# A retention, mixture-of-experts and gated-linear kernel: the first expert's last 64 tokens as stationary operand, and another order of the tile's products

## The chip, the cores and the metric

The kernel runs on one core of a Trainium2 chip. Its time is the device time of one launch in microseconds (us). Before the change three runs gave 780.53, 781.26 and 782.92 us; the median, 781.26 us, is the time to be predicted against. One further execution was profiled, and all rows below are from it.

The engines are named as in the profile: PE is TensorE (matmuls), PEld its loads of the stationary operand, DVE is VectorE, ACT ScalarE, POOL GpSimd, and SP issues most of the DMAs.

## The reference

Three stages follow each other on 2304 tokens (4 sequences of 576) with 512 features.

```python
# 1. retention: 8 heads of 64
scores = (1 / sqrt(64)) * q @ k.T
ret = scores * Dmat            # Dmat[i, j] = gamma_h ** (i - j) for i >= j, else 0
x = (ret @ v) rearranged to (2304, 512)
# 2. mixture of 8 experts, one expert for each token
do_compute = x @ w_skip > 0
e_idx = argmax(x @ w_gate)     # of the tokens with do_compute
gate_w = softmax probability of the chosen expert
h = maximum(x[mask] @ w1[e], 0)            # 512 -> 1024
y[mask] = gate_w * (h @ w2[e])             # 1024 -> 512
x[do_compute] += y
# 3. gated linear unit
out = ((x @ w_a) * (x @ w_b)) @ w_out      # 512 -> 1536 -> 512
```

All is computed in fp32. A fp32 matmul of the program is two matmul instructions in the trace, so that a count of the trace is twice a count of the program.

## The kernel before

**Retention.** The 2304 tokens are 18 tiles of 128 (two sequences are nine tiles: four of the first, four of the second, and one that holds the last 64 tokens of both). For each tile the loop issues, in this order: `scale_k(i + 2)` (POOL multiplies k by a decay, giving `ks`), `scores(i)` (PE, tile `s`; DVE masks them into `At`, L628), transposes of q for a later pair of tiles (`pq`, copied by DVE or ACT), transposes of k for the next tile (`pk`), `emit_x(i - 1)` (PE products `px` of the last tile's result with an identity and the gate's weights, then ACT copies and the store to `x_dram`), `state(i)` (PE product `psm` of k and v, eight 64 x 64 blocks; ACT adds it to the running state `mbd`), and `values(i)`. This last one has a carry part (`po<-qT,mbd`, L663, not in the first tile of a sequence, and L659 in the tile of two halves), an inner part (`po<-At,v`, L668), and a DVE multiplication into `xT`. The DMAs of tile i + 4 are issued behind it. In tiles 1, 6 and 15 a second q transpose stands between `state(i)` and `values(i)`.

`po` of the inner part and `psm` write 64 of the array's 128 columns with one instruction (128*64 in the trace) and `s` reads 64 of its rows (64*128); `pq`, `pk`, `px` and the carry part use the whole array (128*128).

**Routing and the first expert.** Behind some tiles DVE works out the route of the tokens (each expert takes up to `ROOM` = 192 of them). POOL gathers an expert's tokens as 128 and `REST` = 64 rows. The first 128 tokens of expert 0 are gathered from tiles 0 to 14 only, transposed in tile 17 ahead of `values(17)` by `turn_x(0, 0, ...)` (tile `xt`, copied by DVE to `xh`), and their eight first products (`steps`) are spread over the end of the retention, where the routing waits. `firsts` computes a block of 128 of the 1024 hidden features at a time: w1 is stationary (128 x 128), the tokens move. Behind tile 17 two steps run ahead of `emit_x(17)`. Two blocks of hidden features are copied out of PSUM with one ACT instruction (L487).

**Experts.** A branch that reads the number of extra rounds (L961, L962; none are taken with these inputs) follows. Then each expert's instructions are written out by a string of names: F0 to F7 are the first products, S0 to S7 the second ones of 128 tokens (`y`), Q0 to Q7 those of the 64 others (`yr`: tokens stationary, w2 moving in two halves, which go to the lower and the upper 64 columns of the array), X0 and X1 transposes of the next expert's tokens, E0 and E1 the stores, `N` a gather by POOL, `l` a load of expert weights, `tk` a scatter by POOL. `gs` starts and `gp` continues the conversion of a 512 KB piece of the gated unit's weights (ACT and DVE, `hb`, `mh`, `st`, `w`). For expert 0 only F (64 tokens) and Q are left there. All engines run their own instructions strictly in the order written.

**The gated unit** takes the last 400 us and is not touched.

Of the kernel before, what the change touches and what calls it, by code (L numbers as in the profile page):

```python
# [7 lines left out]
F32 = mybir.dt.float32  # L8
# [4 lines left out]
ACTF = mybir.ActivationFunctionType  # L13
# [5 lines left out]
P = 128  # L19
B, H, S, D = 4, 8, 576, 64  # L20
DM = H * D
NP = H // 2
NTOK = B * S
NT = NTOK // P
E = 8
KD = DM // P
F1 = 1024
F2 = 1536
CAP = 256
NBLK = E * CAP // P  # L30
ROOM = 192
# [33 lines left out]
def retention_moe_glu_kernel(  # L65
# [17 lines left out]
    nc = tc.nc  # L83
# [38 lines left out]
    ident = cst[:, C_ID:C_ID + P]  # L122
# [49 lines left out]
    def unit(u, k=3):  # L172
        assert ready.get(u, 0) > k, (u, ready.get(u))
        return units[u]
# [279 lines left out]
    REST = ROOM - P  # L454

    def turn_x(e, b, to, psum, engine):
        n = REST if b else P
        pt = psum([P, KD * n], "xt").rearrange("p (k n) -> p k n", k=KD)
        for kd in range(KD):
            nc.tensor.transpose(pt[:, kd], xg[e][:n, b, kd * P:(kd + 1) * P], ident[:n, :n])  # L460
        if engine is nc.scalar:
            nc.scalar.activation(out=to, in_=pt, func=ACTF.Copy)
        else:
            engine.tensor_copy(to, pt)

    def call(fn, *args):
        return lambda: fn(*args)
# [59 lines left out]
        return [call(second, f) for f in range(8)], finish  # L527


    experts = ExitStack()  # L530
    ps_k = experts.enter_context(tc.tile_pool(name="ps_k", bufs=1, space=PSUM))
    attn = ExitStack()
# [100 lines left out]
    def state(i):  # L633
        c = i % 9
        if c == 8:
            return
        if c % 4 == 0:
            mstate["ps"] = ps_o.tile([P, NP, P], F32, tag="m", name="psm")
        pm = mstate["ps"]
        for hp in range(NP):  # L640
            for r in range(2):
                part = slice(r * D, (r + 1) * D)
                nc.tensor.matmul(pm[part, hp, part], lhsT=ks_t[i][:, 2 * hp + r], rhs=qkv["v", i][:, 2 * hp + r],
                                 start=(c % 4 == 0 and hp == 0), stop=True, skip_group_check=True)
        m = mbd[2 + c // 4] if c % 4 == 3 else mbd[c % 2]
        for r in range(2):
            nc.scalar.activation(out=m[r * D:(r + 1) * D, :, r * D:(r + 1) * D],
                                 in_=pm[r * D:(r + 1) * D, :, r * D:(r + 1) * D], func=ACTF.Copy)
# [63 lines left out]
    for r in range(4):  # L712
# [5 lines left out]
                      in_=w_skip.rearrange("(a p o) -> p a o", p=P, o=1))  # L718
# [79 lines left out]
    for i in range(NT):  # L798
        scale_k(i + 2)
        scores(i)  # L800
        for job in q_jobs[i][:1]:
            q_transposes(*job)
        k_transposes(i + 1)
        emit_x(i - 1)
        state(i)
        route_at(i, "d")
        for job in q_jobs[i][1:]:
            q_transposes(*job)
        if i == NT - 1:
            tags = {"xt": (ps_o, "m"), "h0": (ps_s, "s0"), "h1": (ps_s, "s1"), "y": (ps_k, "o")}  # L810
            tiles = {"ht0": "v", "ht1": "k"}
            xh = at2.tile([P, KD, P], F32, tag="q", bufs=TBUFS["q"], name="xh")

            def early_psum(shape, n):
                return tags[n][0].tile(shape, F32, tag=tags[n][1], name=n)

            def early_sbuf(shape, dt, n):
                return xg[0][:, 0] if n == "yo" else at2.tile(shape, dt, tag=tiles[n], bufs=TBUFS[tiles[n]], name=n)

            ht_0 = {}  # L820
            fs = firsts(0, xh, P, 4, early_sbuf, early_psum, ht_0)
            ss, finish_0 = seconds(0, ht_0, early_sbuf, early_psum)
            steps = fs + ss
            turn_x(0, 0, xh, early_psum, nc.vector)
        values(i)
        load(i + 4)
        route_at(i, "e")
        if 7 <= i:
            for _ in range(1 if i < 14 else 2 if i < NT - 1 else 1):
                load_m()  # L830
        if i == 14:
            zeros = idle_bf.bitcast(F32)
            for j in range(0, ROOM, P):
                n = min(P, ROOM - j)
                for c in range(2):
                    nc.sync.dma_start(out=y_dram[YROWS - ROOM + j:YROWS - ROOM + j + n, c * 256:(c + 1) * 256],
                                      in_=zeros[:n])
    done = 2
    for go in steps[:done]:
        go()  # L840
    emit_x(NT - 1)
    for step, n in enumerate((5, 8, 11, 16)):
# [3 lines left out]
        done = n  # L846
# [115 lines left out]
    with tc.If(rounds > 0):  # L962
        with tc.tile_pool(name="o0", bufs=1) as o0:
            done = o0.tile([P, E], F32, name="done")
# [106 lines left out]
    def prepare_x(e, b):  # L1071
        if e == E:
            return
        if b == 0:
            xe[e] = m1.tile([P, KD, ROOM], F32, tag="xe", bufs=2, name="xe")
        turn_x(e, b, xe[e][:, :, P:] if b else xe[e][:, :, :P], m1_psum(e), nc.vector if b else nc.scalar)
# [6 lines left out]


    FIRST_PLAN = (
        "gs F0 gp F1 gp F2 gp F3 gs E0 F4 gp F5 gp X0 F6 gp F7 gs X1 N l l l l "
        "Q0 Q1 gp Q2 Q3 l l gp Q4 Q5 Q6 gp Q7 l l E1 "
    )
    PLAN = (
        "gs F0 gp F1 tk gp F2 gp F3 gs F4 tk gp F5 gp F6 gp F7 l l l l gs S0 S1 gp S2 "  # L1090
# [3 lines left out]
        "gs F0 f2 gp F1 f1 gp F2 f0 gp F3 gs F4 gp F5 gp F6 x1 gp F7 gs x2 S0 S1 gp t1 S2 "  # L1094
        "x0 S3 gp S4 t2 S5 gp s1 S6 t0 S7 E0 gs s2 Q0 Q1 s0 gp Q2 Q3 gp Q4 Q5 gp Q6 Q7 E1 gs "
    )
    xe = {}
    tokens_put = [0]

    def put_tokens():  # L1100
# [7 lines left out]
    def run_expert(e, plan):  # L1108
        sbuf, psum = m1_sbuf, m1_psum(e)
        acts, ht = {}, {}  # L1110
        if e:
            acts["F"] = firsts(e, xe[e], ROOM, 2, sbuf, psum, ht)
            acts["S"], end_0 = seconds(e, ht, sbuf, psum)
            at = P
        else:
            acts["F"] = firsts(0, xh, REST, 8, sbuf, psum, ht)
            end_0, at = finish_0, 0
        acts["Q"], end_1 = seconds_rest(e, ht, at, sbuf, psum)
        acts["E"] = [end_0, end_1]
        named = {  # L1120
            "N": lambda: gather_x(e + 2), "gp": piece_step,
            "gs": lambda: taken[0] < early and piece_start(),
            "L": piece_load, "l": load_m, "tk": put_tokens,
        }
        uses = {}
        by_tile = {"f": fetch_rows, "x": mix_rows, "t": turn_rows, "s": split_rows}
        for name in plan.split():
            if name in named:
                named[name]()
            elif name[0] == "X":  # L1130
                prepare_x(e + 1, int(name[1]))
            elif name[0] in by_tile:
                by_tile[name[0]](int(name[1]))
            else:
                n = int(name[1])
                acts[name[0]][n]()
                if name[0] in "FSQ":
                    us = [4 * e, 4 * e + 1] if name[0] == "F" else [4 * e + 2 + n // 4]
                    for u in us:
                        uses[u] = uses.get(u, 0) + 1  # L1140
                        if uses[u] == (4 if e == 0 and name[0] == "Q" else 8):
                            used.add(u)

    for e in range(E):
        run_expert(e, FIRST_PLAN if e == 0 else PLAN if e < E - 1 else LAST_PLAN)
    assert loaded["m"] == len(m_pieces)
    experts.close()

# [152 lines left out]
```

## Time and profile before

| what | value |
|---|---|
| median of three runs | 781.26 us |
| profiled execution, whole | 775.75 us |
| its span, first to last instruction | 774.0 us |
| mean granted TensorE clock | 0.986 |
| PE busy | 754.4 us (97%) |
| PEld busy | 662.5 us (86%) |
| DVE, ACT, POOL busy | 305.8, 230.5, 105.6 us |
| the chain that ended last | PE 77%, DVE 4% |

The span's times below count from its first instruction. A busy time of PE covers matmuls that wait in the pipeline, so it says little of how densely the array worked. The start of one group to the start of the next is the better measure of what a group costs. A granted clock of 1.00 in a stretch is 2.4 GHz and 0.50 is 1.2 GHz.

### The profile page before, as it was taken

Reading aid. Unit: us, or ns where it says so; the run is one execution under the profiler, and the core shown is the slowest. Engines: PE = TensorE matmul, PEld = TensorE weight load, DVE = VectorE, ACT = ScalarE, POOL = GpSimd, SP = SyncE. Lnnn points to the kernel's source line nnn. Section 1 sums busy time; section 2 is a strip of 40 time slices with the busy share of each in tenths; the row PEclk is TensorE's granted clock in tenths of the full one; section 3 lists DMA queues with packets and bytes.
Section 4 is the critical chain, followed back from the end, with each engine's and each line's share of the span. In section 5 each row is a group of like instructions: output and inputs, shape, how many; then the busy total and the mean of one; then the engine's idle time right before and its main releaser. Section 6 shows DMA issues by size and latency. Waiting matters only on the chain.

```text
span 774.0 us, 11861 instructions
## 1 busy us (share of the span) xinstructions
PE 754.4 (97%) x4797; PEld 662.5 (86%) x4797; DVE 305.8 (40%) x660; ACT 230.5 (30%) x485; POOL 105.6 (14%) x135
## 2 busy tenths in 40 slices
PE   7999989899999999999999999999999999999997
PEld 5888876877776667988999999999999999999996
DVE  4446664556655136894322221222123222322111
ACT  3444531345444134553221221121112121212111
POOL 1221111202222102140040004000400030001000
PEclk9999999599999999999999999999999999999999
DMA  9979993599898764451030003000301020001001
GB/s 223 228 181 264 254 299 117 180 351 322 304 316 308 260 191 157 130 185 33 1 96 26 1 1 111 13 1 0 123 1 28 14 81 1 1 1 42 1 0 42
DMA packets 89611, 94.61 MB, mean 122 GB/s; under 512 B 44881, under 2 KB 67025, under 8 KB 89554
## 3 DMA queue, kind: packets, MB, share of 16 engines
q1 hardware_dynamic: 84210, 78.06, 33.1%
q0 software_dynamic: 5344, 15.76, 6.4%
q8 instruction: 39, 0.64, 0.3%
q14 instruction: 18, 0.15, 0.1%
HBM read 80.80 MB, written 13.01 MB: 121 GB/s over the span
## 4 chain that ended last, share of the span: by engine, by line
PE 77%; DVE 4%; ACT 0%; issue 0%; POOL 0%; ACTq 0%; DVEq 0%
PE ab L1167 36%; PE o L1184 18%; PE h L484 11%; PE y L498 6%; PE yr L516 4%; PE pt L1050 1%; PE xt L460 1%; DVE w L233 1%; DVE mh L230 1%; DVE mh L225 1%; DVE w L237 0%; DVE hb L234 0%; DVE hb L223 0%; DVE a_sb L1172 0%; ACT gg L445 0%
## 5 line engine op out<-in xcount | busy, mean ns | idle before, releaser
L1167 PE MATMUL ab<-xt,w 128*128 128x384 f32 x1728 | 311.6, 336 | 0.0
L1167 PEld LDWEIGHTS ab<-xt,w 128*128 128x128 f32 x1728 | 301.8, 188 | 6.0 <-issue 0.4
L1184 PE MATMUL o<-w,gg 128*128 128x512 f32 x648 | 161.4, 393 | 1.8 <-ACT gg L445 0.9
L1172 DVE TENSOR_TENSOR a_sb<-ab,a_sb 128x384 f32<-128x384 f32 x72 | 40.1, 557 | 271.8 <-PE ab L1167 239.7
L1184 PEld LDWEIGHTS o<-w,gg 128*128 128x128 f32 x648 | 119.2, 188 | 24.1 <-ACT gg L445 1.8
L1171 ACT ACTIVATE a_sb<-ab 128x384 f32<-128x384 f32 x72 | 35.3, 490 | 174.3 <-PE ab L1167 170.4
L445 ACT ACTIVATE gg<-a_sb 128x384 fp32r<-128x384 f32 x72 | 37.8, 525 | 161.5 <-DVE a_sb L1172 161.5
L484 PEld LDWEIGHTS h<-xe,w 128*128 128x128 f32 x448 | 72.6, 190 | 2.7 <-issue 2.7
L484 PE MATMUL h<-xe,w 128*128 128x192 f32 x448 | 74.7, 328 | 0.0
L498 PE MATMUL y<-w,ht 128*128 128x512 f32 x128 | 59.5, 598 | 0.0
L426 POOL DMA_INDIRECT out_dram<-ob,turns x15 | 14.8, 989 | 310.3 <-ACT ob L1191 308.1
L446 DVE TENSOR_TENSOR gg<-a_sb,gg 128x384 fp32r<-128x384 f32 x68 | 38.0, 559 | 40.2 <-ACT gg L445 37.8
L498 PEld LDWEIGHTS y<-w,ht 128*128 128x128 f32 x128 | 22.8, 190 | 19.9 <-issue 19.2
L233 DVE TENSOR_TENSOR w<-hb,st 128x512 fp32r<-128x512 f32 x36 | 24.8, 690 | 30.5 <-ACT st L228 25.3
L227 ACT ACTIVATE hb<-hb,ebias 128x512 int32<-128x512 int32 x36 | 25.9, 718 | 35.1 <-DVE hb L223 34.8
L487 ACT ACTIVATE ht<-h 128x384 f32<-128x384 f32 (+2 forms) x36 | 16.3, 452 | 55.8 <-PE h L484 54.8
L420 POOL DMA_INDIRECT xg<-x_dram,list_i x15 | 14.7, 982 | 119.3 <-PE xt L460 99.7
L516 PE MATMUL yr<-w,ht 128*64 128x256 f32 x256 | 30.9, 396 | 0.0
L516 PEld LDWEIGHTS yr<-w,ht 128*64 128x64 f32 x256 | 18.3, 142 | 14.4 <-DVE mh L230 3.8
L581 POOL TENSOR_TENSOR ks<-k,cst_a 128x512 f32<-128x512 f32 x18 | 18.8, 1044 | 79.6 <-DMA k<-in_k_dram 64.3
L237 DVE TENSOR_TENSOR w<-mh,hb 128x512 fp32r<-128x512 f32 x36 | 24.4, 688 | 5.3 <-ACT mh L232 3.6
L628 DVE TENSOR_TENSOR At<-s,cst_a 128x512 f32<-128x512 f32 x36 | 23.1, 684 | 6.2 <-PE s L625 6.2
(146 smaller groups left out, 654.3 us busy)
## 6 DMA issues: line engine op xcount, KB each, us to landing
w<-in_moe_w_dram SPq DMA_DIRECT2D x64, 512.0 KB, 6.7
st<-in_moe_w_a_dram SPq DMA_DIRECT2D x12, 512.0 KB
st<-in_moe_w_b_dram SPq DMA_DIRECT2D x12, 512.0 KB, 8.4
st<-in_moe_w_out_dram SPq DMA_DIRECT2D x12, 512.0 KB, 5.5
x_dram<-xs SPq DMA_DIRECT2D x18, 256.0 KB, 4.4
k<-in_k_dram SPq DMA_DIRECT2D x16, 256.0 KB, 4.7
q<-in_q_dram SPq DMA_DIRECT2D x8, 512.0 KB, 5.7
v<-in_v_dram SPq DMA_DIRECT2D x16, 256.0 KB, 5.8
```

The source lines that it names most:

```text
L227: nc.scalar.activation(out=hb, in_=hb, func=ACTF.Relu, scale=8.0, bias=ebias)
L233: nc.vector.tensor_tensor(out=hi, in0=hb.bitcast(F32), in1=wh.bitcast(F32), op=ALU.mult)
L237: nc.vector.tensor_tensor(out=lo, in0=ml, in1=hb.bitcast(F32), op=ALU.mult)
L445: nc.scalar.activation(out=dst_hi, in_=src, func=ACTF.Copy)
L446: lo_engine.tensor_tensor(out=dst_lo, in0=src, in1=dst_hi, op=ALU.subtract)
L484: nc.tensor.matmul(ph[b][:, i], lhsT=w[:, c0:c0 + P], rhs=xh[:, kd], start=(kd == 0), stop=(kd == KD - 1), skip_group_check=True)
L498: nc.tensor.matmul(py[0], lhsT=ht[f][:, :P], rhs=w[:, f % 4], start=(f == 0), stop=(f == 7))
L516: nc.tensor.matmul(py[0][j * REST:(j + 1) * REST], lhsT=ht[f][:, at:at + REST], rhs=w[:, f % 4, j * half:(j + 1) * half], start=(f == 0), ...
L1167: nc.tensor.matmul(p, lhsT=w[a][:, kd, fc:fc + P], rhs=xt2[g][b][kd // 2][:, kd % 2], start=(j == 0), stop=(j == 3 * KD - 1))
L1171: nc.scalar.activation(out=a_sb, in_=pab[0], func=ACTF.Copy)
L1172: nc.vector.tensor_tensor(out=a_sb, in0=pab[1], in1=a_sb, op=ALU.mult)
L1184: nc.tensor.matmul(po[g][t], lhsT=gg[:, a, t * P:(t + 1) * P], rhs=w[b][:, f % 4], start=(f == 0 and j == 0), stop=(f == NF - 1 and j == 2))
```

## The change

- A new function, `firsts_rest`, computes the first products of expert 0's last 64 tokens with the tokens stationary and a row block of w1 moving, in two halves of 512 columns, which go to the two column halves of the array. There are four steps F0 to F3 (one for each 128 input features) in place of eight. One ACT instruction takes the whole result, and `turn` (U0) transposes it back with four PE transposes and one DVE copy.
- In the order of expert 0, X0, X1 and U0 follow F3. The first two steps of expert 1 (G0, G1) stand between U0 and Q0. Expert 1 has an order of its own without F0 and F1. The pieces of the gated unit that are converted are 2 in expert 0 (3 before) and the same 26 in all before the gated unit.
- `state(i)` stands behind `values(i)` in every tile.
- In tile 17 `turn_x(0, 0, ...)` stands behind `values(17)`, and one step of expert 0 in place of two runs ahead of `emit_x(17)`.

```diff
+    def firsts_rest(e, xh, sbuf, psum, ht):
+        got = {}
+
+        def first(kd):
+            if kd == 0:
+                got["ph"] = psum([P, 512], "h")
+            w = unit(("m", 4 * e + kd // 2)).rearrange("p k f -> p (k f)")
+            for j in range(2):
+                c0 = 1024 * (kd % 2) + 512 * j
+                nc.tensor.matmul(got["ph"][j * REST:(j + 1) * REST], lhsT=xh[:, kd], rhs=w[:, c0:c0 + 512],
+                                 start=(kd == 0), stop=(kd == KD - 1), skip_group_check=True)
+            if kd == KD - 1:
+                got["h"] = sbuf([P, 8 * REST], F32, "ht")
+                nc.scalar.activation(out=got["h"], in_=got["ph"], func=ACTF.Relu)
+
+        def turn():
+            pt = psum([P, DM], "xt").rearrange("p (k n) -> p k n", k=4)
+            for k in range(4):
+                nc.tensor.transpose(pt[:, k], got["h"][:, k * P:(k + 1) * P], ident)
+            t = sbuf([P, DM], F32, "yo").rearrange("p (k n) -> p k n", k=4)
+            nc.vector.tensor_copy(t, pt)
+            for k in range(8):
+                ht[k] = t[:, k % 4, k // 4 * REST:(k // 4 + 1) * REST]
+
+        return [call(first, kd) for kd in range(KD)], turn
...
         emit_x(i - 1)
-        state(i)
         route_at(i, "d")
         for job in q_jobs[i][1:]:
             q_transposes(*job)
...
             steps = fs + ss
+        values(i)
+        state(i)
+        if i == NT - 1:
             turn_x(0, 0, xh, early_psum, nc.vector)
-        values(i)
         load(i + 4)
...
-    done = 2
+    done = 1
...
     FIRST_PLAN = (
-        "gs F0 gp F1 gp F2 gp F3 gs E0 F4 gp F5 gp X0 F6 gp F7 gs X1 N l l l l "
-        "Q0 Q1 gp Q2 Q3 l l gp Q4 Q5 Q6 gp Q7 l l E1 "
+        "gs F0 F1 gp F2 F3 X0 gp X1 N U0 gp G0 E0 gs G1 l l l l Q0 Q1 gp Q2 Q3 gp l l Q4 Q5 gp Q6 Q7 l l E1 "
+    )
...
-            acts["F"] = firsts(0, xh, REST, 8, sbuf, psum, ht)
+            acts["F"], turn = firsts_rest(0, xh, sbuf, psum, ht)
+            acts["U"] = [turn]
...
-        uses = {}
+        uses = {4 * e: 2, 4 * e + 1: 2} if e == 1 else {}
...
+            elif name[0] == "G":
+                if e + 1 not in begun:
+                    h = {}
+                    begun[e + 1] = firsts(e + 1, xe[e + 1], ROOM, 2, sbuf, m1_psum(e + 1), h), h
+                begun[e + 1][0][int(name[1])]()
...
-                        if uses[u] == (4 if e == 0 and name[0] == "Q" else 8):
+                        if uses[u] == (8 if e else 4):
```

PE's order in tile 12 of the retention, from its transposes on. Before:

```order
L591 MATMUL pq<-cst,q 128x128 x4
L613 MATMUL pk<-cst,ks 128x128 x4
L693 MATMUL px_1193<-xl_rhs,xT 128x137 x2
L693 MATMUL px_1197<-xl_rhs,xT 128x137 x2
L643 MATMUL psm<-v,ks 64x64 x8
L663 MATMUL po<-qT,mbd_126 128x128 x4
L668 MATMUL po<-At,v 64x128 x8
```

After:

```order
L619 MATMUL pq<-cst,q 128x128 x4
L641 MATMUL pk<-cst,ks 128x128 x4
L721 MATMUL px_1193<-xl_rhs,xT 128x137 x2
L721 MATMUL px_1197<-xl_rhs,xT 128x137 x2
L691 MATMUL po<-qT,mbd_126 128x128 x4
L696 MATMUL po<-At,v 64x128 x8
L671 MATMUL psm<-v,ks 64x64 x8
```

The state product `psm` moved from between two groups that use the whole array to behind the inner part, which writes 64 columns as it does.

PE's order behind the branch, in expert 0 and at the start of expert 1 (`h<-xh,w` and `h<-w,xh` are expert 0's 64 tokens, `h<-xe,w` is expert 1). Before:

```order
L484 MATMUL h_2033<-xh,w 128x64 x24
L460 MATMUL xt<-cst,xg 128x128 x4
L484 MATMUL h_2033<-xh,w 128x64 x8
L460 MATMUL xt<-cst,xg 128x64 x4
L516 MATMUL yr<-w,ht_2034 64x256 x16
L484 MATMUL h_2161<-xe,w 128x192 x8
L484 MATMUL h_2182<-xe,w 128x192 x8
```

After:

```order
L540 MATMUL h<-w,xh 64x512 x8
L460 MATMUL xt<-cst,xg 128x128 x4
L460 MATMUL xt<-cst,xg 128x64 x4
L549 MATMUL xt<-cst,ht 128x128 x4
L484 MATMUL h_2076<-xe,w 128x192 x8
L516 MATMUL yr<-w,yo 64x256 x16
L484 MATMUL h_2139<-xe,w 128x192 x8
```

Thirty-two matmuls of 64 columns became eight of 512, four transposes (L549) came in, and expert 1's first eight matmuls moved ahead of `yr`.

PE's order in tile 17 and behind it (`xt` are expert 0's first 128 tokens, `h` their first products; the other rows of `po<-qT`, which alternate between two states, read alike). Before:

```order
L693 MATMUL px_1609<-xl_rhs,xT 128x137 x2
L460 MATMUL xt<-cst,xg 128x128 x4
L659 MATMUL po<-qT,mbd_128 128x64
...
L668 MATMUL po<-At,v 64x128 x8
...
L484 MATMUL h_1648<-xh,w 128x128 x8
L693 MATMUL px_1660<-xl_rhs,xT 128x137 x2
L693 MATMUL px_1665<-xl_rhs,xT 128x137 x2
L484 MATMUL h_1648<-xh,w 128x128 x8
L484 MATMUL h_1691<-xh,w 128x128 x4
```

After:

```order
L721 MATMUL px_1609<-xl_rhs,xT 128x137 x2
L687 MATMUL po<-qT,mbd_128 128x64
...
L696 MATMUL po<-At,v 64x128 x8
L460 MATMUL xt<-cst,xg 128x128 x4
...
L484 MATMUL h_1648<-xh,w 128x128 x4
L721 MATMUL px_1655<-xl_rhs,xT 128x137 x2
L721 MATMUL px_1660<-xl_rhs,xT 128x137 x2
L484 MATMUL h_1648<-xh,w 128x128 x12
L484 MATMUL h_1691<-xh,w 128x128 x4
```

The transposes `xt` moved behind the tile's values, and one step of four matmuls moved from ahead of `px` to behind it.

## Rows read from the trace of the kernel before

**Rows 1.** Busy time by stretch around expert 0 (first line: the columns)

```profile
core 0: us, PE busy (x) PEld busy (x) DVE busy (x) ACT busy (x) POOL busy (x), PEclk, DMA share, GB/s
110.18:117.96 7.78, 5.65 (x63) 5.11 (x62) 3.00 (x6) 0.80 (x2) 0.55 (x1) 1.00 0.74 242
...
135.94:138.11 2.17, 2.16 (x16) 1.97 (x16) 2.00 (x14) 0.39 (x1) 0.00 (x0) 0.87 0.02 4
139.21:142.88 3.67, 3.67 (x16) 3.48 (x16) 3.15 (x6) 0.47 (x1) 0.00 (x0) 0.50 0.50 140
...
151.63:156.69 5.06, 5.06 (x33) 2.83 (x32) 3.10 (x6) 1.89 (x3) 1.47 (x3) 0.70 0.96 337
```

**Rows 2.** PE in time, expert 0's last tokens: start, length, instruction, [idle before]

```profile
135.94 2.17 PE L484 MATMUL h<-xh,w 128*128 128x64 f32 x16 [1.06 <-DVEq L962]
139.21 3.67 PE L484 MATMUL h<-xh,w 128*128 128x64 f32 x16 [1.11 <-ACT ht L487]
...
151.63 5.13 PE L516 MATMUL yr<-w,ht 128*64 128x256 f32 x32
156.69 8.55 PE L484 MATMUL h<-xe,w 128*128 128x192 f32 x51
```

**Rows 3.** PE in time, expert 2's second products and expert 3's first ones

```profile
191.87 0.60 PE L460 MATMUL xt<-cst,xg 128*128 128x128 f32 x4
192.31 1.88 PE L498 MATMUL y<-w,ht 128*128 128x512 f32 x4
...
197.28 3.67 PE L516 MATMUL yr<-w,ht 128*64 128x256 f32 x32
200.88 10.67 PE L484 MATMUL h<-xe,w 128*128 128x192 f32 x64
```

**Rows 4.** Page, part 5: yr's stationary loads; busy, mean ns, idle before

```profile
L516 PEld LDWEIGHTS yr<-w,ht 128*64 128x64 f32 x256 | 18.3, 142 | 14.4 <-DVE mh L230 3.8
```

**Rows 5.** PE in time, around the states of tiles 8, 9 and 10

```profile
59.55 1.10 PE L693 MATMUL px<-xl_rhs,xT 128*128 128x137 f32 x8
60.50 1.89 PE L659 MATMUL po<-qT,mbd 128*128 128x64 f32 x16
...
66.40 0.69 PE L643 MATMUL psm<-v,ks 128*64 128x64 f32 x16
66.92 1.04 PE L668 MATMUL po<-At,v 128*64 128x128 f32 x16
...
69.91 1.10 PE L693 MATMUL px<-xl_rhs,xT 128*128 128x137 f32 x8
70.94 0.69 PE L643 MATMUL psm<-v,ks 128*64 128x64 f32 x16
71.56 1.16 PE L663 MATMUL po<-qT,mbd 128*128 128x128 f32 x8
```

**Rows 6.** PE in time: a wait in tile 2 and one in tile 6

```profile
24.76 0.63 PE L591 MATMUL pq<-cst,q 128*128 128x128 f32 x4 [1.49 <-DMA q<-in_q_dram]
...
49.27 0.43 PE L591 MATMUL pq<-cst,q 64*128 64x64 f32 x4 [0.19 <-DVE qT L599]
```

**Rows 7.** All engines in time, tile 17 and what follows it

```profile
111.27 1.21 PE L693 MATMUL px<-xl_rhs,xT 128*128 128x137 f32 x8
...
114.61 0.63 PE L460 MATMUL xt<-cst,xg 128*128 128x128 f32 x4 [2.13 <-DMA xg<-x_dram,list]
...
115.07 1.90 PE L659 MATMUL po<-qT,mbd 128*128 128x64 f32 x16
115.27 0.69 DVE L464 COPY xh<-xt 128x512 f32<-128x512 f32 x1 [2.11 <-PE xt L460]
...
117.96 2.03 PE L484 MATMUL h<-xh,w 128*128 128x128 f32 x16
118.04 0.76 DVE L676 TENSOR_TENSOR xT<-po,qt_sb 128x256 f32<-128x256 f32 x2 [2.08 <-PE po L668]
...
125.21 2.05 PE L484 MATMUL h<-xh,w 128*128 128x128 f32 x16 [0.52 <-ACT ht L487]
```

More of the change, by code (lines that the diff above doesn't have):

```diff
@@ L1085, in retention_moe_glu_kernel @@
     FIRST_PLAN = (
-        "gs F0 gp F1 gp F2 gp F3 gs E0 F4 gp F5 gp X0 F6 gp F7 gs X1 N l l l l "
-        "Q0 Q1 gp Q2 Q3 l l gp Q4 Q5 Q6 gp Q7 l l E1 "
+        "gs F0 F1 gp F2 F3 X0 gp X1 N U0 gp G0 E0 gs G1 l l l l Q0 Q1 gp Q2 Q3 gp l l Q4 Q5 gp Q6 Q7 l l E1 "
+    )
+    SECOND_PLAN = (
+        "gs F2 tk gp F3 gp F4 tk gp F5 gs F6 gp F7 l l l l gp S0 S1 gp S2 "
+        "X0 S3 gs S4 X1 N gp S5 gp S6 S7 tk gp E0 Q0 gs Q1 Q2 gp Q3 l l Q4 gp Q5 Q6 gp Q7 l l E1 "
     )
@@ L1096, in retention_moe_glu_kernel @@
     )
-    xe = {}
+    xe, begun = {}, {}
     tokens_put = [0]
@@ L1111, in run_expert @@
         if e:
-            acts["F"] = firsts(e, xe[e], ROOM, 2, sbuf, psum, ht)
+            if e not in begun:
+                begun[e] = firsts(e, xe[e], ROOM, 2, sbuf, psum, ht), ht
+            acts["F"], ht = begun[e]
             acts["S"], end_0 = seconds(e, ht, sbuf, psum)
@@ L1140, in run_expert @@
                         uses[u] = uses.get(u, 0) + 1
-                        if uses[u] == (4 if e == 0 and name[0] == "Q" else 8):
+                        if uses[u] == (8 if e else 4):
                             used.add(u)
     for e in range(E):
-        run_expert(e, FIRST_PLAN if e == 0 else PLAN if e < E - 1 else LAST_PLAN)
+        run_expert(e, FIRST_PLAN if e == 0 else SECOND_PLAN if e == 1 else PLAN if e < E - 1 else LAST_PLAN)
     assert loaded["m"] == len(m_pieces)
```

## The prediction

> **What bounds the kernel now.** I read the cores' view first (span 774.0 us, one core), then PE's row of the busy times: 97%, while DVE has 40% and ACT 30%. The chain of waits is PE for 77% of the span. So time can only come from PE's own work, its gaps or its clock. The stretches by granted clock show where the last two lie. All the retention up to tile 17 reads 1.00 [rows 1], but around expert 0 the clock falls: 0.87 in 135.94 to 138.11, 0.50 behind it, 0.70 in 151.63 to 156.69. From these shares, the fall is at about 137.5 (a share x at half speed gives 1 - x/2 = 0.87, so 0.56 of 2.17 us) and the return at about 154.7. That is 17 us at 1.2 GHz. PE's view in time tells what ran there [rows 2]: expert 0's last 64 tokens, 16 matmul instructions of 64 columns in 2.17 us and, at the lower clock, 16 in 3.67 us, with gaps of 1.06 us (the branch) and 1.11 us (a copy by ACT). The clock came back 3 us into `yr`, whose two halves fill the array. The busy row hides all this, since a matmul that crawls counts as busy.
>
> **The change, part by part.**
>
> *Expert 0 behind the branch.* Before, from the first `h` at 135.94 to expert 1's first product at 156.69 are 20.75 us [rows 2]. After, the same stretch holds 16 instructions of 512 columns, 12 transposes, `yr`, and expert 1's first 16 instructions, which are only moved and count nothing. The price of a 512-column instruction that shares the array with its twin has no row. The nearest is `yr` in expert 2 at full clock: 32 instructions of 256 columns between the starts 197.28 and 200.88, 0.1125 us each [rows 3]. Twice the columns give 0.225, and 16 of them 3.60 us. Four transposes take 0.44 us (191.87 to 192.31 [rows 3]), three groups 1.32 us, and the 64-row group surely not more. `yr` takes 3.60 us. The sum is 8.52 us, a gain of 12.2 us. It supposes the full clock, for which I argue below.
>
> The new waits: U0 must wait for ACT's copy of the whole result. For a copy of 128 x 512 I take DVE's 0.69 us [rows 7]; X0 and X1 stand before U0 with 0.88 us and cover it. U0's own DVE copy, the same 0.69, lies beside G0 and G1. Not covered is what is queued ahead on ACT and DVE: the conversion of a weight piece stands between F1 and F2, and behind X0. That queue made the 1.11 us gap of before [rows 2]. Now 3.6 us of PE work run before its result is wanted. Bounds are 0 and 1.11; I take 0.3, nearer to nothing because the cover is three times as long. If X0's gather were late, the copy's 0.69 us would show too. POOL's gathers and scatters keep their order; SP has the same eight weight loads in this expert, two pieces of the gated unit's weights come behind some of them, and the pieces done before the gated unit remain 26. So nothing is owed later there.
>
> *State behind values.* Between groups that use the array alike, PE goes on faster. From `px` to the carry part are 0.95 us (59.55 to 60.50), from `px` to `psm` 1.03 [rows 5]. From `psm` to the carry part are 0.62, from `psm` to the inner part, of the same width, 0.52. So a tile with a carry part can gain 0.08 + 0.10 = 0.18 us. There are 12 such tiles. Tile 1's share goes into the wait for q's DMA in tile 2 [rows 6]. In tiles 6 and 15 the second q transposes wait for DVE's copy, 0.19 us with `psm` ahead of them [rows 6]; with `psm` gone from there the wait only grows, and `psm` comes on top, 0.52 us lost in each. Nine times 0.18 less twice 0.52 makes +0.6. The other tiles where PE waits for DVE keep their cover, since the state of the tile before now lies there. Bounds: all twelve gain, +2.2; tiles 11 and 16, which also have routing work on DVE, lose theirs as well, -0.8. Queued behind the later `psm` are the carry part of the next tile (it needs `mbd` from ACT) and the scaling of k on POOL. Scores, transposes and `px` lie between, over 2.5 us, so I charge nothing; without that cover it would be the two ACT copies of a state. SP's load of a later v waits for `psm` too, four tiles ahead of its use.
>
> *Tile 17.* PE stands 2.13 us for the gather [rows 7]. The tile's values, 115.07 to 117.96, are 2.9 us of work that can fill it, so the gap goes. What is late next is `xh`: DVE, in order, first multiplies `xT` (0.08 us behind the values, 0.76 long), then copies `xh` (0.69), which puts the first product 1.57 us behind the values, with 0.48 us of transposes and a small product in it: a new gap of 1.1. And with one step ahead of `px` in place of two, the third step meets ACT's copy of the first two, as the one at 125.21 did: 0.52 us [rows 7]. Together 2.13 - 1.1 - 0.5 = +0.5, with 0 (xh later still) and 1.6 (no second wait) as ends.
>
> **Sum.** 12.2 - 0.3 + 0.6 + 0.5 = 13.0 us. The profiled execution took 775.75 us with a span of 774.0, so it would take 762.7. The median of the timed runs is 5.5 us above it, by something no row shows; taking that as unchanged gives **768.3 us**.
>
> **A rule against it.** In `yr` of expert 2 a pair of instructions costs 0.225 us, while the load of 64 stationary columns lasts 0.142 us on average [rows 3, 4]: two loads alone are longer than the whole pair, so most of them are hidden. The Trainium skill ("TensorE: Matmul & The Clock Gate", The mechanism) says that a load overlaps running matmuls only when its row group differs. The two column halves share their rows, so by it each load would stand free, which is the first rival below; by the trace it would not.
>
> **The rivals.**
>
> *The stationary loads are not hidden.* Sixteen loads at 0.142 us add 2.3: 770.6 us. Against it stands the pair's price in `yr`; for it, that the moving operand is longer and untried here.
>
> *The clock still falls, for a short time.* For it: the branch's gap of 1.06 us and the few columns before it remain, and it fell 1.6 us behind that gap. Against: behind the gap now comes dense work, like the `yr` that brought the clock back. If it falls at the same place, 2.0 us of `h` take 4.0, and the return comes with the transposes: about 2.5 us lost, 770.8 us.
>
> *The clock stays low until G0.* Then the transposes (1.3) and 3 us of the dense work behind them also run at half speed: 2.0 + 1.3 + 1.5 = 4.8 us lost, 773.1 us. For it: four copies and transposes in a row are not dense. Against: they are 1.3 us only.
>
> *The transfers cannot follow.* The DMA engines were busy for 0.96 of 151.63 to 156.69 [rows 1]. If the weights of expert 1 and the pieces to convert only come when they came before, PE waits at expert 1 behind ACT's conversions and gives the 12 us back: 780 us. Against: expert 1's first products have their weights from the retention.
>
> *Slower.* The two new gaps in tile 17, 1.1 and 0.52 us, push the clock down there, and it stays low to the branch. Products from 117.96 to 135.94, less the gap, are 16.9 us [rows 2, 7], which would double: 785.2 us. It becomes slower than before from 13 us of work at half clock on. Against: with a single gap of 2.13 us at this very place the clock read 1.00 [rows 1].
>
> **How the numbers follow.** Forecast 0.62 (766 to 770); short fall 0.17; low until G0 0.09; loads 0.04; transfers 0.05; slower 0.03. A measurement of this kernel tells about 0.3% (2.3 us) from no change. The first four are faster, 0.92; the transfers are the same, 0.05; the last is 0.03. The range reaches up past the clock's second case, to 774.5, and down to 764.5: the states' upper bound (1.6 more), no second wait in tile 17 (1.1) and a part of the unexplained 5.5 us, should it be more time at the low clock in the timed runs.
>
> **What would show it.** Right: 16 `h` instructions of 512 columns in about 3.6 us behind the branch; granted clock 1.00 from there to expert 1; expert 1's third step about 10 us nearer to the first `h`; no 2.13 us wait in tile 17, but one of about 1.1 for `xh` and one of 0.5 for ACT; `px` to the carry part 0.95. Wrong: a clock of 0.5 over more than 4 us, a pair of `h` above 0.6 us at full clock, U0 or G0 waiting over 1 us, or a DMA named as what expert 1 waits for.

## The result, and the profile after

The changed kernel takes **772.46 us** (median of 4 runs, 770.08 to 774.81), beside 782.09 (780.53 to 784.58, 4 runs) before: a ratio of 0.989, with a 95% interval of 0.9858 to 0.9921. Forecast were 768.3, in a range of 764.5 to 774.5. The time is in the range, 4.2 us above the point; of the 13.0 us of saving, 9.6 came. In the table of runs below, one run of `rest_only`, 781.44 us, counts as slow and is left out.

The stretches of the changed kernel, in the view of busy time by stretch (columns: ends and length of the stretch; busy time and count of PE, PEld, DVE, ACT, POOL; granted TensorE clock; DMA share; GB/s):

```profile
core 0: us, PE busy (x) PEld busy (x) DVE busy (x) ACT busy (x) POOL busy (x), PEclk, DMA share, GB/s
110.11:118.00 7.89, 7.03 (x77) 6.49 (x74) 3.61 (x10) 1.55 (x4) 0.09 (x1) 1.00 0.72 243
118.00:135.36 17.36, 15.29 (x94) 10.59 (x93) 6.94 (x38) 2.44 (x7) 2.77 (x3) 1.00 0.35 109
135.36:139.00 3.64, 3.64 (x17) 1.28 (x17) 3.10 (x15) 1.30 (x2) 0.00 (x0) 1.00 0.01 2
139.00:146.97 7.97, 7.95 (x61) 5.88 (x60) 5.39 (x11) 4.30 (x8) 0.69 (x1) 1.00 0.78 259
146.97:156.00 9.03, 9.03 (x53) 8.48 (x52) 6.30 (x13) 5.02 (x9) 3.50 (x6) 1.00 1.00 349
...
172.00:176.00 4.00, 0.00 (x0) 0.00 (x0) 3.54 (x8) 1.83 (x4) 0.00 (x0) 1.00 1.00 378
176.00:178.00 2.00, 0.88 (x3) 0.88 (x4) 1.57 (x4) 1.96 (x5) 0.00 (x0) 0.51 0.76 197
178.00:182.50 4.50, 4.50 (x16) 4.50 (x15) 3.16 (x6) 1.29 (x2) 0.00 (x0) 0.50 0.87 284
```

Where [rows 1] had 0.87, 0.50 and 0.70 around expert 0, the clock now reads 1.00 from the branch to 156. A new low stands behind it, 0.51 and 0.50 in 176 to 182.5; PE did nothing in the 4 us before. PE in time shows both places (start, length, instruction, count, [idle before and what ended it]):

```profile
135.36 3.65 PE L540 MATMUL h<-w,xh 128*64 128x512 f32 x16 [1.07 <-DVEq L991]
138.95 1.04 PE L460 MATMUL xt<-cst,xg 128*128 128x128 f32 x8
139.92 0.66 PE L549 MATMUL xt<-cst,ht 128*128 128x128 f32 x4
140.60 2.84 PE L484 MATMUL h<-xe,w 128*128 128x192 f32 x16
143.37 3.67 PE L516 MATMUL yr<-w,yo 128*64 128x256 f32 x32
146.97 8.07 PE L484 MATMUL h<-xe,w 128*128 128x192 f32 x48
...
177.12 8.28 PE L484 MATMUL h<-xe,w 128*128 128x192 f32 x32 [5.19 <-ACT ht L487]
...
193.22 3.03 PE L516 MATMUL yr<-w,ht 128*64 128x256 f32 x26
```

From the first `h` to expert 1's third step are 11.61 us, where 20.75 us led to its first step alone [rows 2]. Expert 1's `yr` begins 12.33 us earlier than in the first profile of before (162.86 for 175.19). But expert 2's begins only 4.06 earlier (193.22 for 197.28). Expert 2's first products wait 5.19 us for ACT and then take 8.1 us from start to start (177.12 to 185.24) instead of some 5.25 for 32 instructions. What ACT did before that:

```profile
171.44 0.72 ACT L227 ACTIVATE hb<-hb,ebias 128x512 int32<-128x512 int32 x1 [7.87 <-DVE hb L223]
...
175.41 0.72 ACT L227 ACTIVATE hb<-hb,ebias 128x512 int32<-128x512 int32 x1 [2.17 <-DVE hb L223]
176.04 0.66 ACT L228 ACTIVATE st<-st 128x512 f32<-128x512 int32 x1
176.59 0.47 ACT L487 ACTIVATE ht<-h 128x384 f32<-128x384 f32 x1
```

and DVE, at the first step of each piece of the gated unit's weights:

```profile
152.88 0.43 DVE L223 TENSOR_SCALAR hb<-st 128x512 int32<-128x512 int32 x1 [1.27 <-DMA st<-in_moe_w_a_dram]
160.50 0.43 DVE L223 TENSOR_SCALAR hb<-st 128x512 int32<-128x512 int32 x1 [3.69 <-DMA st<-in_moe_w_b_dram]
170.98 0.43 DVE L223 TENSOR_SCALAR hb<-st 128x512 int32<-128x512 int32 x1 [6.73 <-DMA st<-in_moe_w_b_dram]
```

Read upwards, this is the chain. `ht` (176.59) needs only `h`, but stands in ACT's order behind two pieces' conversions; these stand behind DVE; and DVE stood 6.73 us for a piece that the DMA had not brought. The three waits grow, 1.27, 3.69, 6.73: the backlog adds up. The late piece was there at 170.98. PE ran out of work at 171.9 and then waited for the conversions of this piece and the next. In 140 to 170 a piece took 12.0 us from issue to landing (median of four, 512 KB each), and 9.1 in the same window before (DMA issues; before, then after):

```profile
st<-in_moe_w_b_dram SPq DMA_DIRECT2D x4, 512.0 KB, 9.1
st<-in_moe_w_b_dram SPq DMA_DIRECT2D x4, 512.0 KB, 12.0
```

In 146 to 172 the DMA engines were nearly full in both kernels (shares of 0.89 to 1.05). Before, their share then fell to 0.46 (busy time by stretch, before):

```profile
172.00:178.00 6.00, 6.00 (x37) 3.30 (x38) 3.36 (x7) 2.29 (x4) 4.31 (x7) 1.00 0.46 145
```

After, the work of that pause is wanted 12 us sooner. From 135 to expert 1's `yr` the DMA engines had moved 10.42 MB before and only 8.09 MB after, though 12 loads of expert weights were issued in it in both and five pieces in place of six.

Later another 2.3 us goes: expert 7's `yr` is 1.75 us ahead and no longer 4.05. Most of it is that a transpose of gathered rows waits 1.96 us (299.54, for DVE's `pair`), which before it did not. Then the gated unit's second products wait 2.6 us for `gg` instead of 1.7.

**The profile of before was a low one.** Those ledgers end 1.0 us apart (774.0 and 773.0), the medians 9.6. The profiled execution of before took 775.75 us, while its timed runs here lie between 780.5 and 784.6. That of after, 774.81 us, was the slowest of its four. A second profile of the unchanged kernel, `before_copy` below, shows what the first had been spared.

### The profile page after: what moved, and what is told of

Its sections match the earlier page's. It is cut to its first block, busy times and chain, and to the rows that moved or that the text cites. A ratio compares the mean times of both kernels' runs of the same rounds, so it can differ in the third digit from the quotient of the medians.

```text
span 773.0 us, 11780 instructions
## 1 busy us (share of the span) xinstructions
PE 744.8 (96%) x4753; PEld 653.9 (85%) x4753; DVE 306.8 (40%) x661; ACT 231.0 (30%) x482; POOL 105.9 (14%) x135
## 4 chain that ended last, share of the span: by engine, by line
PE 72%; DMA 6%; DVE 2%; issue 1%; ACT 1%; POOL 0%; SPq 0%; DVEq 0%; POOLq 0%
PE ab L1207 37%; PE o L1224 18%; PE h L484 7%; PE y L498 5%; PE yr L516 3%; DMA st<-in_moe_w_b_dram 2%; DMA w<-in_moe_w_dram 2%; DMA st<-in_moe_w_out_dram 1%; PE pt L1079 1%; DMA pair<-y_dram,turns 1%; PE xt L460 1%; DVE w L233 0%; PE h L540 0%; DVE mh L230 0%; DVE hb L223 0%
## 5 line engine op out<-in xcount | busy, mean ns | idle before, releaser
L484 PE MATMUL h<-xe,w 128*128 128x192 f32 x448 | 78.0, 336 | 5.2 <-ACT ht L487 5.2
L484 PEld LDWEIGHTS h<-xe,w 128*128 128x128 f32 x448 | 75.4, 196 | 8.4 <-ACT ht L487 5.5
L498 PEld LDWEIGHTS y<-w,ht 128*128 128x128 f32 x128 | 22.8, 190 | 19.9 <-issue 19.0
L487 ACT ACTIVATE ht<-h 128x384 f32<-128x384 f32 (+1 forms) x32 | 15.2, 475 | 43.4 <-PE h L484 43.4
L516 PEld LDWEIGHTS yr<-w,ht 128*64 128x64 f32 x224 | 15.5, 137 | 12.4 <-DVE mh L230 3.8
L516 PE MATMUL yr<-w,ht 128*64 128x256 f32 x224 | 25.7, 382 | 0.0
```

The lines of the kernel that those rows point to most:

```text
L484: nc.tensor.matmul(ph[b][:, i], lhsT=w[:, c0:c0 + P], rhs=xh[:, kd], start=(kd == 0), stop=(kd == KD - 1), skip_group_check=True)
L498: nc.tensor.matmul(py[0], lhsT=ht[f][:, :P], rhs=w[:, f % 4], start=(f == 0), stop=(f == 7))
L516: nc.tensor.matmul(py[0][j * REST:(j + 1) * REST], lhsT=ht[f][:, at:at + REST], rhs=w[:, f % 4, j * half:(j + 1) * half], start=(f == 0), ...
```

## The experiments

All numbers are us; before was run with each group.

| run | median (range, runs) | ratio to before, 95% |
|---|---|---|
| `rest_only` | 776.64 (768.38–778.24, 11) | 0.992 (0.9892–0.9948) |
| `order_only` | 775.92 (774.32–777.35, 6) | 0.9928 (0.9908–0.9949) |
| `late_pieces` | 765.2 (763.71–766.28, 5) | 0.9786 (0.9763–0.981) |
| `after_copy` | 772.56 (768.18–774.29, 6) | 0.9865 (0.9836–0.9895) |
| `tile17_only` | 777.38 (776.87–778.73, 12) | 0.9959 (0.9936–0.9983) |
| `state_only` | 779.77 (775.57–781.97, 12) | 0.999 (0.9966–1.0013) |
| `mixed` | 763.9 (762.89–766.81, 6) | 0.98 (0.9764–0.9835) |
| `before_copy` | 780.93 (single run) | – |
| `one_half` | 777.92 (single run) | – |
| `filler` | 775.14 (774.26–778.1, 8) | 0.9926 (0.99–0.9953) |
| `mixed_t1` | 764.57 (763.73–767.56, 6) | 0.9794 (0.9766–0.9822) |
| `late_copy` | 765.54 (763.07–767.47, 6) | 0.9793 (0.9766–0.9821) |

**The kernels as they are** (`after_copy`, `before_copy`, no edit).

> The changed kernel once more, to have another profile of it on the same chip as the other three. Theory 1: a wait of PE for ACT ht of 3 us or more at expert 2 again, ratio to before 0.986 to 0.992. Theory 2 (accident): no such wait, or one elsewhere.

> The kernel before once more, for a second profile. Theory 1: about 781 us, the clock at 0.50 for some 7 us behind the wait for the gather in tile 17, and as in the first profile behind the branch. Theory 2: the 5 us lie elsewhere (DMA waits of the first tiles, the experts).

`after_copy` repeats the changed kernel: 5.91 us of wait in expert 2 at 177.91, clock 0.57 in 176 to 184. This low is not in every execution. Two of the six timed runs have a mean granted clock of 1.000 and 0.998, too high for 7 us at half clock, and took 768.18 and 768.66 us; the four others have 0.993 to 0.997 and took 771.69 to 774.29. The fastest run of `rest_only`, 768.38 us, also has 1.000.

`before_copy` has a span of 779.2. Its retention is 1.6 us later at tile 17 (0.6 by tile 3, 0.6 in tile 11, where DVE is late, and a `px` wait of 0.40), and then this happens (PE in time, and the stretches behind it):

```profile
116.23 0.63 PE L460 MATMUL xt<-cst,xg 128*128 128x128 f32 x4 [2.09 <-DMA xg<-x_dram,list]
```

```profile
112.00:116.00 4.00, 1.74 (x18) 1.37 (x16) 2.10 (x4) 0.80 (x2) 0.00 (x0) 1.00 0.81 299
116.00:120.00 4.00, 3.77 (x28) 3.68 (x30) 0.69 (x1) 0.00 (x0) 0.00 (x0) 0.73 0.64 183
120.00:124.00 4.00, 4.00 (x27) 3.67 (x24) 1.15 (x5) 0.00 (x0) 0.00 (x0) 0.50 0.00 0
124.00:128.00 4.00, 4.00 (x34) 4.00 (x34) 1.95 (x11) 1.57 (x4) 0.00 (x0) 0.92 0.11 32
```

The wait for the gather is as long as in [rows 7], 2.09 for 2.13 us, but the clock falls behind it, to 0.50, for some 7 us. The low behind the branch, 17 us long in the first profile, lasts 13.7 here, and from the first `h` to expert 1 are 19.94 us in place of 20.75; `order_only`, `tile17_only` and `state_only` have 19.9 too. The first `h` behind the branch stands at 140.74 and not 135.94: 1.6 come from earlier in the retention, 3.2 from here. Against this pair of profiles the ledger reads: 5.3 us ahead at the branch (140.74 to 135.42), 16.25 at expert 1's `yr` (179.17 to 162.92), 7.5 at expert 2's (201.27 to 193.75), 6.7 at the end. So +5.3, +10.9, -8.7, -0.8.

**The change in two parts.** `rest_only` is the changed kernel with this undone:

```diff
         emit_x(i - 1)
+        state(i)
...
-        values(i)
-        state(i)
-        if i == NT - 1:
             turn_x(0, 0, xh, early_psum, nc.vector)
+        values(i)
...
-    done = 1
+    done = 2
```

`order_only` is the kernel before with just these lines as the change has them.

> The changed kernel with the retention's order of before (state ahead of values, tile 17's transposes ahead of its values, two steps ahead of px); only the new first products of expert 0 and the new orders of experts 0 and 1 are kept. Theory 1 (the gain is made at expert 0, 11.7 us, and part of it is lost at expert 2, because the pieces of the gated unit's weights land too late): first h behind the branch at 135.9 us, expert 1's yr 11.7 us earlier than before (near 163.5), again a wait of PE for ACT ht in expert 2, and a time within 1.5 us above the changed kernel. Theory 2 (the order of the retention's products matters as much as expert 0): the time lies at least 3 us above the changed kernel.

> The kernel before with state behind values, tile 17's transposes behind its values and one step ahead of px; expert 0 as before. Theory 1: 0.6 us are gained up to the branch (first h near 135.4) and nothing else, ratio to before 0.998 to 1.001. Theory 2: ratio to before 0.995 or less.

The expert's part alone is worth 4.6 us by the medians (781.23 to 776.64) and the order's 5.3 (775.92); together 9.9, and the whole change 8.7 in that group. Both runs came out as their second theory had it: the order counts about as much as expert 0. In `rest_only` the first `h` to `yr` take 8.01 us (140.54, 148.55), as after; the wait in expert 2 is there too (4.68 us at 181.79), and so is the low clock in tile 17 (0.62 in 116 to 120, 0.52 in 120 to 124). In `order_only` no gather wait is left, tile 17 reads 1.00, and the low clock behind the branch stays (0.50 in 140 to 152). The first `h` of `rest_only` had been expected at 135.9, from the one profile of before in which that clock held; of the 4.6 us, 3.2 come from this low and 1.4 from earlier in the retention.

**Tile 17 alone, the states alone.** Each is the kernel before with one edit:

```diff
-            turn_x(0, 0, xh, early_psum, nc.vector)
         values(i)
+        if i == NT - 1:
+            turn_x(0, 0, xh, early_psum, nc.vector)
...
-    done = 2
+    done = 1
```

```diff
-        state(i)
         route_at(i, "d")
...
         values(i)
+        state(i)
```

> The kernel before with tile 17's transposes behind its values and one step ahead of px; states and expert 0 as before. Theory 1 (in most runs of the kernel before, the wait of 2.1 us for the gather in tile 17 brings the clock down for some 7 us, as in the profile of rest_only, and that is the part by which its timed runs lie above its one profile): 4 to 6 us under before, ratio 0.992 to 0.995, no wait for the gather, clock 1.00 in tile 17. Theory 2 (the wait costs its 2.1 us at most and gives back 1.6, as predicted): 0 to 1 us under before, ratio 0.9985 to 1.0.

> The kernel before with state behind values in every tile; tile 17 and expert 0 as before. Theory 1 (the gain of the retention's order is tile 17's): within 1 us of before, the wait for the gather in tile 17 stays. Theory 2 (the states' order carries the 5 us by which order_only is faster): 4 us or more under before. In both, a tile with a carry part takes 0.35 us less than in the profile of before, tiles 6, 11 and 15 take 0.45 to 0.75 us more.

`tile17_only` saves 3.2 us, between what its two theories expected. Its waits are 0.86, 0.47 and 0.52, and the clock holds:

```profile
116.00:120.00 4.00, 3.14 (x34) 2.73 (x34) 1.75 (x6) 0.00 (x0) 0.00 (x0) 1.00 0.67 199
120.00:124.00 4.00, 3.53 (x31) 3.34 (x30) 1.95 (x11) 1.18 (x3) 0.00 (x0) 1.00 0.38 85
```

Behind the three short gaps the clock stayed at 1.00, while behind the one of 2 us it fell in four traces of five: most of what the edit brings is the clock. The waits alone went from 2.13 to 0.86 and 0.47, 0.8 us less; the low alone cost 3.2 us in `before_copy`. `state_only` saves 0.8 us, which its interval does not tell from nothing; a gather wait of 2.69 and clocks of 0.58 and 0.56 behind it (116 to 124) remain. So of `order_only`'s 5.3, 3.2 come with tile 17 alone and 0.8 with the states alone; where the other 1.3 lie, within the runs' spread or in the two together, is not shown.

**Fewer pieces right behind the fast stretch** (`late_pieces`, and again as `late_copy`): expert 1 converts two pieces of the gated unit's weights instead of four, expert 2 three instead of four, and experts 5 and 6 the three that are then missing of the 26 (each `gs` begins a piece). Shown is expert 1's part:

```diff
...
-        "gs F2 tk gp F3 gp F4 tk gp F5 gs F6 gp F7 l l l l gp S0 S1 gp S2 "
-        "X0 S3 gs S4 X1 N gp S5 gp S6 S7 tk gp E0 Q0 gs Q1 Q2 gp Q3 l l Q4 gp Q5 Q6 gp Q7 l l E1 "
+        "F2 tk F3 F4 tk gs F5 gp F6 gp F7 l l l l gp S0 S1 S2 "
+        "X0 S3 gs S4 X1 N gp S5 gp S6 S7 tk gp E0 Q0 Q1 Q2 Q3 l l Q4 Q5 Q6 Q7 l l E1 "
...
```

> The changed kernel with 2 pieces of the gated unit's weights converted in expert 1 and 3 in expert 2, in place of 4 and 4; the 3 others come in experts 5 and 6, still 26 ahead of the gated unit. Theory 1 (the pieces' loads cannot follow the faster expert 0, and ACT's copies of h stand queued behind their conversion): no wait of PE above 1 us in expert 2, the clock there stays at 1.00, expert 2's yr 12 us earlier than in the profile of before (near 185), and a time 4 to 8 us under the changed kernel. Theory 2 (that wait and the low clock behind it are an accident of the one profiled run, or have another cause than the loads): the time of the changed kernel within 1.5 us.

> late_pieces once more, on the chip of mixed_t1: 765.2 us within 1 us, no wait above 1 us in expert 2, clock 1.00 there. If mixed's states are worth nothing, mixed_t1 is less than 1.7 us under it.

765.2 us, 7.4 under `after_copy` in the same group, the wait and the low clock of expert 2 gone (PE in time):

```profile
162.49 3.67 PE L516 MATMUL yr<-w,ht 128*64 128x256 f32 x32
166.09 10.67 PE L484 MATMUL h<-xe,w 128*128 128x192 f32 x64
176.60 2.74 PE L498 MATMUL y<-w,ht 128*128 128x512 f32 x6
...
184.58 3.67 PE L516 MATMUL yr<-w,ht 128*64 128x256 f32 x32
```

From `yr` to `yr` are 22.09 us, as in before (175.19 to 197.28), where the changed kernel needs 30.36. So 8.3 us of the gain were given back there, and the pieces are the cause. Whether it is their bytes or their conversions the edit alone does not tell, since it defers both. That it begins with the bytes is read from DVE's waits, which are waits for a landing: between 130 and 260 they were 12.6 us in three, 6.7 the longest, for pieces of one matrix (`after`), and in `late_pieces`

```profile
DVE hb L223 <- DMA st<-in_moe_w_b_dram: 1.5, 2, 1.4
```

The DMA engines moved as much in 140 to 170 as in the changed kernel (10.88 MB for 10.75), with one piece fewer among it.

**Do the halves run side by side?** `one_half` puts both halves into the same 64 columns of the array, with two PSUM tiles and two copies (shown is the product alone):

```diff
...
-                nc.tensor.matmul(got["ph"][j * REST:(j + 1) * REST], lhsT=xh[:, kd], rhs=w[:, c0:c0 + 512],
+                nc.tensor.matmul(got["ph"][j][:REST], lhsT=xh[:, kd], rhs=w[:, c0:c0 + 512],
...
```

> The changed kernel with both halves of expert 0's new first products in the same 64 columns of the array (two PSUM tiles, two ACT copies), so that no two of them can run side by side; the work is the same. Theory 1 (the two column halves run at once, and the loads of the tokens are hidden): the 16 instructions of h behind the branch take 6.8 to 7.3 us from start to start in place of 3.6. Theory 2 (the long rows alone make the gain): 3.6 to 4.2 us. Open: whether the clock holds with half of the columns in use.

```profile
135.29 7.05 PE L540 MATMUL h<-w,xh 128*64 128x512 f32 x16 [1.07 <-DVEq L992]
142.27 1.05 PE L460 MATMUL xt<-cst,xg 128*128 128x128 f32 x8
```

Start to start, the 16 instructions take 6.98 us and not 3.59: the halves run side by side. An instruction costs 0.436 us by itself, and one of each half together 0.449, so 0.224 each. The loads are hidden as well (PEld's group in the changed kernel, 135.3 to 139):

```profile
L540 PEld LDWEIGHTS h<-w,xh 128*64 128x64 f32 x16 | 1.3, 136 | 2.7 <-issue 2.7
```

Sixteen loads of 0.136 us, standing free, would have added 2.2 us to the 3.59. And a pair of 512 columns costs twice a pair of 256 in `yr` (0.449 for 0.225), with as many loads in it, so nothing is left that a load adds. The Trainium skill ("TensorE: Matmul & The Clock Gate", The mechanism) says that a load overlaps running matmuls only when the row group differs; the same section also lets a load for the background weight buffer go ahead. The trace disagrees with the first: the two halves share their rows, and a pair takes 0.449 us with its two loads. In `one_half` the clock stayed at 1.00 from the branch to expert 2 too.

**Does the clock hold with more products in the same place?** `filler` is the kernel before, with two bf16 products of 512 columns, whose result nobody reads, behind each of expert 0's eight steps of 64 tokens.

```diff
...
+            if n < P:
+                if f == 0:
+                    fill.append(psum([P, DM], "xt"))
+                keep_warm(fill[0], 2)
...
```

> The kernel before with two dense products of 512 columns in bf16, whose result nobody reads, behind each of expert 0's eight steps of 64 tokens: more work, 3.4 us at full clock. Theory 1 (the clock falls there because the 64-column products keep the array too empty): the clock stays at 1.00 from the branch to expert 1, the stretch from the first h to expert 1's first product falls from 20.75 to about 15 to 17 us, and the time is 3 to 5 us under before. Theory 2 (the gaps of the branch and of ACT's copies bring it down, or it falls whatever stands there): the clock falls as before and the time is 3 us or more above before.

```profile
141.47 1.08 PE L485 MATMUL h<-xh,w 128*128 128x64 f32 x8 [1.07 <-DVEq L967]
142.38 0.59 PE L127 MATMUL xt<-idle_bf 128*128 128x512 bf16 x2
...
144.75 1.10 PE L485 MATMUL h<-xh,w 128*128 128x64 f32 x8 [0.50 <-ACT ht L492]
...
153.60 3.67 PE L521 MATMUL yr<-w,ht 128*64 128x256 f32 x32
157.20 3.03 PE L485 MATMUL h<-xe,w 128*128 128x192 f32 x17
```

Sixteen more products, and yet 775.14 us, 6.1 under before (3 to 5 were expected): the stretch takes 15.73 us (141.47 to 157.20) instead of 20.75, or 19.94 in `before_copy`, at a granted clock of 1.00 throughout. The branch's gap of 1.07 us was there too. But the edit changes two things at once: there is more work in the stretch, and the added products run while ACT copies, so that the waits for ACT are 0.50 us in place of 1.11 and 0.37. Which of the two kept the clock is not shown. What before shows is that the low can last without a gap: in 143.25 to 151.63 PE was busy all the time, at 0.50.

**What is still to be had.** `mixed` is `late_pieces` with the state ahead of the values again in five tiles, at or next to those where PE waits for DVE, and `mixed_t1` has in addition one step `t1` of expert 7 two steps later.

```diff
+COVER = (0, 1, 6, 11, 15)
...
+        if i in COVER:
+            state(i)
         route_at(i, "d")
...
-        state(i)
+        if i not in COVER:
+            state(i)
```

```diff
-        "... gs x2 S0 S1 gp t1 S2 "
-        "x0 S3 gp S4 t2 S5 ..."
+        "... gs x2 S0 S1 gp S2 "
+        "x0 S3 gp t1 S4 t2 S5 ..."
```

> late_pieces with state ahead of values again in the tiles 0, 1, 6, 11 and 15, where the second q transposes or the inner part wait for DVE. Theory (state is worth its place ahead where PE waits, and behind where it does not): 1 to 2 us under late_pieces, 763.5 to 764.5 us if late_pieces is again at 765.2. Rival (DVE's chains start later by what is gained, so the order there is worth nothing): within 0.5 us of late_pieces.

> mixed with the gated unit's second transposes of tokens (t1) two steps of expert 7 later. Theory: the wait of 1.7 us for the gathered rows there goes, 762 to 763 us, 1 us or more under mixed and 2 us or more under late_copy. Rival: the wait moves to the next group, and the time is mixed's (763.9 us) within 0.5 us.

Medians of 763.9, and 764.57 beside 765.54 of `late_copy`: within the runs' spread, so neither edit is shown to be worth anything. `mixed` lies 1.3 us under `late_pieces`, as expected, but in another group of runs; `mixed_t1` is not under `mixed` by the 1 us expected. The wait in expert 7 moved on rather than went. In `mixed` it is 1.70 us; in `mixed_t1`:

```profile
289.34 0.66 PE L1083 MATMUL xt<-cst,pair 128*128 128x128 f32 x4 [0.39 <-DVE pair L1068]
291.27 0.66 PE L1083 MATMUL xt<-cst,pair 128*128 128x128 f32 x4 [0.42 <-DVE pair L1068]
294.73 0.77 PE L1083 MATMUL xt<-cst,pair 128*128 128x128 f32 x4 [1.08 <-DVE xt L447]
```

The best version is thus `late_pieces` or either of these, 2.0 to 2.1% under before. Why the gathered rows come late in expert 7 stays open.

## Why the prediction came out as it did

**Expert 0, 12.2 - 0.3 us: right.** Measured are 11.75: expert 1's `yr` is 12.33 ahead of the first profile, and 0.58 of that was there at the branch (135.94 to 135.36). Against `before_copy`, whose low was shorter, it is 10.9. Each of the 16 instructions cost 0.224 us (0.225 taken from `yr`), the loads were hidden, U0 did not wait, and the clock did not fall. The 0.3 us set aside for waits went into the transposes, 1.65 us (138.95 to 140.60) for 1.32. The argument for the clock was that dense work now follows the branch's gap; `filler` agrees, without telling the work from the shorter waits. One reading was too wide: "All the retention up to tile 17 reads 1.00" holds from 15 us on; in 5 to 10 the granted clock was 0.79 and in 10 to 15 0.87.

**Tile 17, +0.5 us: the waits right, the worth wrong.** Foreseen were new gaps of 1.1 (the 1.57 in its sum is 1.53 by its own terms, which leaves 1.1) and 0.5 instead of 2.13; they are 0.86 and 0.47 (PE in time, changed kernel):

```profile
115.10 0.66 PE L460 MATMUL xt<-cst,xg 128*128 128x128 f32 x4
...
116.62 1.16 PE L484 MATMUL h<-xh,w 128*128 128x128 f32 x8 [0.86 <-DVE xh L464]
117.62 1.10 PE L721 MATMUL px<-xl_rhs,xT 128*128 128x137 f32 x8
118.56 1.05 PE L484 MATMUL h<-xh,w 128*128 128x128 f32 x8
120.09 2.94 PE L484 MATMUL h<-xh,w 128*128 128x128 f32 x24 [0.47 <-ACT ht L487]
```

The sentence that failed is "with a single gap of 2.13 us at this very place the clock read 1.00". It was true of one execution. Of five traces that have this wait (the first of before, `before_copy`, `rest_only`, `state_only`, `filler`), the clock falls behind it in four. The edit is worth 3.2 us by itself. It is probably also the larger part of the 5.5 us "by something no row shows" by which before's median lay above its profile: in `before_copy` 3.2 of the 4.8 us by which the branch is later come from there.

**States, +0.6 us: mis-sized in its parts, about right in sum** (0.48 from tile 3's scores to tile 17's). From the start of one tile's scores to the next, a tile with a carry part went from 5.78 to 5.43 us, 0.35 and not 0.18. All the steps of its chain changed: from `px` to `psm`, the carry part, the inner part and the next scores were 1.03, 0.62, 1.09 and 1.02, in sum 3.76; from `px` to the carry part, the inner part, `psm` and the scores are now 0.95, 0.98, 0.93 and 0.56, in sum 3.42. I had priced only the first two.

```profile
69.72 1.10 PE L721 MATMUL px<-xl_rhs,xT 128*128 128x137 f32 x8
70.67 1.05 PE L691 MATMUL po<-qT,mbd 128*128 128x128 f32 x8
71.65 1.09 PE L696 MATMUL po<-At,v 128*64 128x128 f32 x16
72.58 0.63 PE L671 MATMUL psm<-v,ks 128*64 128x64 f32 x16
...
78.84 0.43 PE L696 MATMUL po<-At,v 128*64 128x128 f32 x2 [1.36 <-DVE At L656]
```

`px` to the carry part is 0.95, as forecast from [rows 5]. On the other side tiles 6 and 15 lose 0.47 and 0.46 (0.52 each forecast), and tile 11 loses 0.73, its inner part waiting 1.36 us for DVE (last row). That tile was in the bound, not in the sum. `state_only`'s 0.8 agrees with 0.6 and is not told from zero.

**The rival with 0.05 is what took the gain.** "The transfers cannot follow" was priced at the whole 12 us and set aside because "expert 1's first products have their weights from the retention". They had. The step that failed is the last one on expert 0's edit, "So nothing is owed later there": it counted the loads and did not ask where the pause in the DMA's work had been. The stretch lost 12 us, with nearly the same loads to bring in it; the delay came one expert later, not through expert 1's weights but through the conversions queued on DVE and ACT ahead of expert 2's `ht`. It cost 8.3 us in the profiled execution: 5.2 of waiting and, the rest, the low clock behind the wait.

So the point was near for a reason it did not have. Between the second profiles, 5.3 us up to the branch and 10.9 for expert 0, less 8.7 for the transfers and 0.8 behind them, leave 6.7 us; the medians are 8.7 to 9.6 apart, and the rest lies in the spread of single executions.

**The other rivals.** Clock falling behind the branch for a short time, or until G0: no, 1.00 in every trace with `firsts_rest`. Loads not hidden: no, 3.59 us and not 5.9 for the 16 instructions. Low clock through tile 17's gaps: no, 1.00 in tile 17 wherever the three short gaps stand.

## What to carry to other kernels

When a stretch becomes shorter, add up the bytes that have to arrive during it and find the pause in the DMA's work that had absorbed them; then follow every engine's in-order queue from the transfer that is late to the first instruction the bounding engine needs. A gap's price on PE is its length plus the clock behind it, and one profile that kept its clock does not prove that the next will: compare the profile's own time with the median first. A stage that is busy all the time can be slow by its clock, as expert 0 was at 0.50: read the granted clock beside the busy share. Here two edits brought it to 1.00, the operands swapped and products added whose result nobody read.

## What the runs showed that I had not expected

- Sixteen bf16 products of 512 columns, whose results nobody read, made a stretch of 64-column fp32 products faster, 15.73 us for 20.75, with a granted clock of 1.00 throughout, where before it read 0.50 for 17 us (`filler`).
- Behind a wait of 2.0 to 2.7 us in the same place the clock fell to 0.50 (1.2 GHz) for some 7 us in four traces of five and not in the fifth; behind the gaps of 0.9 and 0.5 us that took its place it did not.
- Moving one group of products behind another of the same width saved 0.35 us of 5.78 in a tile with the same products; that it is the width is argued and not shown apart.
